# A fused attention and gMLP kernel: batch 0 loaded and attended pair by pair, its gMLP moved ahead, dummy matmuls, and two batches stored from another queue

## Chip, cores, metric

The kernel runs on one core of one Trainium2 chip. The metric is device time in microseconds (us); lower is better. All times compared here are of runs in the same (fast) state; runs in the slow state are left out of the ratios. A ratio is the mean time of one kernel's fast runs divided by the mean of the other's fast runs of the same rounds, so it is not quite the ratio of the medians that are quoted beside it.

## The reference

Sliding-window causal attention (window 64) over q, k, v of shape (8, 8, 576, 64) in float32, then a gMLP block with a spatial gate on the (8, 576, 512) result:

```python
scores = where(0 <= i - j < 64, q @ k.T / 8, -1e9)           # per batch and head
x = softmax(scores) @ v                                      # heads side by side: 8 x 576 x 512
h = maximum(x @ w_in, 0);  u, v = h[..., :512], h[..., 512:]
v_n = (v - mean(v)) / sqrt(var(v) + 1e-6)
v_s = einsum('ts,bsd->btd', w_spatial, v_n) + b_spatial[None, :, None]
out = (u * v_s) @ w_out                                      # 8 x 576 x 512
```

## The kernel before

All work is written out in a fixed order, and each engine runs its instructions in that order. Per batch b there are five attention steps s (four pairs of heads, then the remaining 64 rows of all heads). The letters used below:

- T(b,s): PE transposes q and k; VectorE copies them from PSUM, where PE's products go, to SBUF, where the tiles lie. S: scores. E: ScalarE's exp, then VectorE's min with a mask. P(b,s): PE's product with v. N1, N2: ScalarE's log and exp of the sums, then VectorE's x.
- V(b,j): five tiles of the v half of `x @ w_in`. LN: VectorE normalises them in five operations `vn`. U and G: the u half and the spatial product with the gate. O(b,j): the output product; ScalarE copies it to an output buffer `ob`, and a DMA stores it.
- GpSimd casts q, k, v of the next batch to float16 and makes `hs`, a copy of v shifted by 64 rows, with five copies. P needs it.

`ob` has three buffers; from batch 1 on all loads of q, k and v, and all stores, are issued by SyncE in program order; and loads run two batches ahead. The code below is condensed, with cuts marked by dots.

```python
def emit_O(b, j):
    ...                                                   # four matmuls into po
    ob = mpool.tile([128, 512], f32, tag="ob", bufs=3, name=f"ob{b}_{j}")
    nc.scalar.copy(ob[0:jn, :], po[0:jn, :])
    nc.sync.dma_start(out[b, 128 * j:128 * j + jn, :], ob[0:jn, :])
...
for p in range(4):                                        # batch 0: all casts come first, so
    cast_pair(0, 1, p, nc.gpsimd)                         # VectorE has four q casts in front of
    cast_pair(0, 0, p, nc.vector)                         # the first copy of a transpose
    cast_pair(0, 2, p, nc.gpsimd)
    shift_pair(0, p, nc.gpsimd)
...
for i in range(B + 2):            # attention of i, V/LN/U/G of i-1, O of i-2
    ...
    if i == 0: loads += [(1, x, c) ...]                   # 15 chunks of 256 KB
    if i + 2 < B: loads += [(i + 2, x, c) ...]            # two batches ahead
    for s in range(5):
        ...                       # load_chunk on SyncE; casts of batch i+1 on GpSimd
        emit_T(next step); two units of todo (V, U, G, O)
        emit_S(i, s); emit_P(previous step)
        ...                       # E, N1, N2 with one unit of todo between each
```

The softmax here doesn't subtract the row's maximum and nothing guards it: scores larger than these inputs give would overflow.

## Time and profile before

| | before |
|---|---|
| median of the first three runs | 266.21 us (266.09 to 266.33) |
| span of the profiled run | 265.3 us |
| PE busy | 217.4 us (82%) |
| start of P(2,0), the first P of batch 2 | 92.07 us |
| from there to the end | 173.2 us |
| V(b,0) to V(b+1,0), b = 2 to 6 | 25.5 us |

P(2,0) is used throughout as a mark: it splits the start of the program from its steady part.

The page is the profiler's summary of one execution. It cuts the span into 40 slices (one digit is the busy share, or the clock granted to PE, of 6.6 us in tenths). Its chain of waits is followed back from the last instruction, at each step to what released it; SPq is SyncE issuing DMAs. For the kernel before:

```profile
PE   0008325999990499999999999999999999999893
...
PEclk9999655599997599999999999999999999999999
DMA  8999999999999699869966995597320040005005
...
PE 64%; SPq 16%; DMA 9%; POOL 6%; issue 1%; ACT 1%; DVE 0%; ACTq 0%; POOLq 0%
```

Apart from its end, PE has holes in slices 0 to 6 and 12 to 13 only. Its granted clock reads 5 tenths in slices 5 to 7 and 13. And the DMA row stands at 9 until slice 12: in that stretch the chain of waits is mostly made of SyncE's issues and of DMAs (SPq and DMA, 25% of the whole together), the rest of GpSimd's casts and shifts (POOL, 6%).

The windows view (stretch, its length, busy us of each engine with the number of instructions, granted clock, DMA share, GB/s):

```profile
core 0: us, PE busy (x) PEld busy (x) DVE busy (x) ACT busy (x) POOL busy (x), PEclk, DMA share, GB/s
...
35.00:40.00 5.00, 1.60 (x6) 0.63 (x6) 0.00 (x0) 0.00 (x0) 4.49 (x8) 0.50 1.23 216
...
80.00:85.00 5.00, 0.00 (x0) 0.00 (x0) 0.00 (x0) 0.00 (x0) 2.61 (x5) 0.83 1.00 204
85.00:90.00 5.00, 0.30 (x1) 0.10 (x1) 0.00 (x0) 0.93 (x3) 4.71 (x6) 0.50 0.85 239
```

PE does nothing at all for five microseconds while the DMA moves 204 GB/s. What it waits for is in three timelines of the same kernel (start, duration, engine, line, operation; in brackets the idle time before it and its releaser). PE first:

```profile
78.86 0.38 PE L311 MATMUL pv_0_1231<-win_189,x_3_1098 128*128 128x512 f16 x1
89.70 0.58 PE L311 MATMUL pv_1_1242<-win_183,x_0_766 128*128 128x512 f16 x1 [10.46 <-ACT ob_3_1195 L387]
...
92.07 0.64 PE L262 MATMUL oz_0_1271<-e_2_0_1175,onesK 128*64 128x512 f16 x2
```

The second V tile of batch 1 comes 10.46 us late; its PSUM buffer is released by ScalarE's copy of `ob_3`. ScalarE:

```profile
76.02 0.59 ACT L387 COPY ob_2_1184<-po_2_1178 128x512 f32<-128x512 f32 x1 [0.16 <-PE po_2_1178 L384]
...
89.07 0.59 ACT L387 COPY ob_3_1195<-po_3_1189 128x512 f32<-128x512 f32 x1 [12.18 <-DMA out_dram<-ob_0_1133]
```

That copy waits 12.18 us for the store of `ob_0`, whose buffer it reuses. SyncE's issues:

```profile
81.42 3.06 SPq L76 DMA_DIRECT2D nk_1105<-in_k_dram  x3
84.58 1.24 SPq L388 DMA_DIRECT2D out_dram<-ob_0_1133  x1
```

The store of `ob_0`, ready at 74.1, is issued at 84.58, behind loads of batch 4. Batch 2's data were there by then, as GpSimd's timeline shows (last v chunk cast, fourth shift copy):

```profile
67.46 0.80 POOL L88 CAST hv_593<-nv_353 64x512 f16<-64x512 f32 x1 [0.22 <-DMA nv_353<-in_v_dram]
...
71.49 1.04 POOL L104 COPY hs_594<-hv_593 64x1024 f16<-64x1024 f16 x1
```

### The profile page before, as it was taken

The numbers are of one execution on the slowest core, as the hardware profiler recorded it, in microseconds if no ns is written. First come the engines' busy times: TensorE is split into PE (matmuls) and PEld (weight loads), VectorE is DVE, ScalarE is ACT, GpSimd is POOL, SyncE is SP. The second block draws the span as 40 slices with busy tenths as digits, with TensorE's granted clock in tenths as the row PEclk, the third lists the DMA queues.
The fourth block names the chain that finished last, engine by engine and source line by source line (L and its number), as shares of the span: only waits on it lengthen the run. The fifth ranks groups of instructions, "written<-read, shape, count | busy, mean of one in ns | idle before, by whom it ended". The sixth has DMA issues, their size and how long they took to land.

```text
span 265.3 us, 6260 instructions
## 1 busy us (share of the span) xinstructions
PE 217.4 (82%) x2537; PEld 114.1 (43%) x2537; DVE 155.3 (59%) x316; ACT 149.7 (56%) x262; POOL 120.6 (45%) x183
## 2 busy tenths in 40 slices
PE   0008325999990499999999999999999999999893
PEld 0006203644640245544554455445544644454351
DVE  5125402598740377759766976697578648863730
ACT  1006502766640467577667767776876777776423
POOL 4579384795885607670866087417830000000000
PEclk9999655599997599999999999999999999999999
DMA  8999999999999699869966995597320040005005
GB/s 161 210 195 208 207 210 200 183 207 203 200 195 203 201 200 207 134 216 211 183 153 199 191 217 144 167 215 139 115 68 0 2 160 20 4 2 180 0 2 178
DMA packets 119822, 40.41 MB, mean 152 GB/s; under 512 B 113584, under 2 KB 114672, under 8 KB 119792
## 3 DMA queue, kind: packets, MB, share of 16 engines
q1 hardware_dynamic: 113200, 36.58, 67.9%
q0 software_dynamic: 1840, 2.24, 4.8%
q10 hardware_dynamic: 4752, 1.18, 2.7%
q8 instruction: 20, 0.33, 0.6%
q14 instruction: 10, 0.08, 0.1%
HBM read 32.79 MB, written 9.44 MB: 159 GB/s over the span
## 4 chain that ended last, share of the span: by engine, by line
PE 64%; SPq 16%; DMA 9%; POOL 6%; issue 1%; ACT 1%; DVE 0%; ACTq 0%; POOLq 0%
SPq L76 14%; DMA nq_76<-in_q_dram 4%; DMA nv_353<-in_v_dram 2%; DMA nv_229<-in_v_dram 2%; DMA out_dram<-ob_0_1133 2%; SPq L68 2%; POOL hk_592 L88 1%; POOL hk_1101 L88 1%; POOL hs_233 L103 1%; POOL hs_233 L104 1%; POOL hs_594 L104 1%; POOL hs_594 L103 1%; PE pv_1_1242 L311 1%; PE ps_0_4499 L363 1%; PE ps_0_2533 L363 1%
## 5 line engine op out<-in xcount | busy, mean ns | idle before, releaser
L245 ACT ACTIVATE e_0_0_275<-sc_0_257 128x1024 f16<-128x1024 f32 x1 | 1.0, 1025 | 19.2 <-PE sc_0_257 L223 19.2
L191 PE MATMUL tp_1_245<-id_110,hk_80 128*128 128x128 f16 x4 | 0.6, 302 | 11.0 <-DVE qk_0_225 L197 11.0
L311 PE MATMUL pv_1_1242<-win_183,x_0_766 128*128 128x512 f16 x1 | 0.6, 585 | 10.5 <-ACT ob_3_1195 L387 10.5
L191 PEld LDWEIGHTS <-hk_80 128*128 128x128 f16 x16 | 1.5, 129 | 17.4 <-issue 9.5
L81 DVE CAST hq_79<-nq_76 128x512 f16<-128x512 f32 x4 | 1.9, 481 | 10.9 <-DMA nq_76<-in_q_dram 10.9
L289 DVE TENSOR_TENSOR x_4_1200<-oz_4_1163,zi_4_1198 128x256 f16<-128x256 f32 x1 | 0.4, 425 | 12.8 <-ACT zi_4_1198 L287 12.8
L249 ACT ACTIVATE e2r_547<-sc_4_509 128x512 f16<-128x512 f32 x1 | 0.6, 597 | 12.5 <-PE sc_4_509 L237 12.5
L88 POOL CAST hk_1655<-nk_1105 128x512 f16<-128x512 f32 (+1 forms) x5 | 2.8, 610 | 10.5 <-issue 10.5
L387 ACT COPY ob_3_1195<-po_3_1189 128x512 f32<-128x512 f32 x1 | 0.6, 586 | 12.2 <-DMA out_dram<-ob_0_1133 12.2
L197 DVE COPY qk_0_507<-tp_0_497 128x1024 f16<-128x1024 f16 x1 | 0.7, 693 | 11.4 <-PE tp_0_497 L194 11.4
L191 PE MATMUL tp_0_497<-id_110,hk_231 128*128 128x128 f16 x4 | 1.2, 288 | 7.2 <-POOL hk_231 L88 7.2
L262 PEld LDWEIGHTS <-onesK 128*64 128x64 f16 x80 | 4.8, 108 | 5.1 <-issue 2.5
L88 POOL CAST hk_3317<-nk_2767 128x512 f16<-128x512 f32 (+1 forms) x5 | 2.9, 610 | 8.6 <-issue 8.6
L88 POOL CAST hk_2763<-nk_2213 128x512 f16<-128x512 f32 (+1 forms) x5 | 2.8, 609 | 8.6 <-issue 8.6
L88 POOL CAST hk_2209<-nk_1659 128x512 f16<-128x512 f32 (+1 forms) x5 | 2.8, 610 | 8.6 <-issue 8.6
L81 POOL CAST hk_80<-nk_77 128x512 f16<-128x512 f32 x4 | 2.4, 612 | 7.7 <-DMA nk_77<-in_k_dram 7.7
L191 PE MATMUL tp_0_215<-id_110,hk_80 128*128 128x128 f16 x4 | 0.6, 305 | 5.8 <-POOL hk_80 L81 5.8
L311 PEld LDWEIGHTS <-x_1_882 128*128 128x128 f16 x4 | 0.4, 104 | 10.9 <-issue 10.7
L191 PEld LDWEIGHTS <-hk_231 128*128 128x128 f16 x16 | 1.3, 115 | 8.4 <-POOL hk_231 L88 7.8
L88 POOL CAST hv_593<-nv_353 128x512 f16<-128x512 f32 (+1 forms) x5 | 3.6, 719 | 2.7 <-DMA nv_353<-in_v_dram 2.6
L343 PEld LDWEIGHTS <-win_187 128*128 128x128 f16 x32 | 3.1, 98 | 3.8
L343 PEld LDWEIGHTS <-win_189 128*128 128x128 f16 x32 | 3.1, 98 | 3.8
(1855 smaller groups left out, 952.9 us busy)
## 6 DMA issues: line engine op xcount, KB each, us to landing
nk_77<-in_k_dram SPq DMA_DIRECT2D x9, 128.0 KB, 4.6
nv_78<-in_v_dram ACTq DMA_DIRECT2D x9, 128.0 KB, 4.7
nq_76<-in_q_dram SPq DMA_DIRECT2D x9, 128.0 KB, 4.5
nk_228<-in_k_dram SPq DMA_DIRECT2D x4, 256.0 KB, 5.5
nq_227<-in_q_dram SPq DMA_DIRECT2D x4, 256.0 KB, 14.7
nv_229<-in_v_dram SPq DMA_DIRECT2D x4, 256.0 KB, 6.0
nk_352<-in_k_dram SPq DMA_DIRECT2D x4, 256.0 KB, 6.0
nq_351<-in_q_dram SPq DMA_DIRECT2D x4, 256.0 KB, 5.3
```

Of the source, the lines that this page charges most:

```text
L68: eng.dma_start(NAT[b][x][:, 0:4, h, :], SRC[x][b, h, 0:512, :].rearrange("(c p) d -> p c d", p=128))
L76: nc.sync.dma_start(NAT[b][x][0:sn, c, :, :], SRC[x][b, :, 128 * c:128 * c + sn, :].transpose([1, 0, 2]))
L81: eng.tensor_copy(F16[b][x][:, 0:4, hs, :], NAT[b][x][:, 0:4, hs, :])
L88: eng.tensor_copy(F16[b][x][0:sn, c, :, :], NAT[b][x][0:sn, c, :, :])
L103: eng.tensor_copy(vs[0:64, c:c + 2, :, :], vn[0:64, c:c + 2, :, :])
L104: eng.tensor_copy(vs[64:128, c + 1:c + 3, :, :], vn[64:128, c:c + 2, :, :])
L191: nc.tensor.transpose(tp[:, 512 + 128 * c:640 + 128 * c], Kh[:, c, 2 * s:2 * s + 2, :], id16[:, :])
L245: nc.scalar.activation(e2[:, :, :], sc[:, :, :], AF.Exp, bias=0.0, scale=0.125)
L262: nc.tensor.matmul(oz[64 * h:64 * h + 64, 1, 0:n], onesK[:, :], e2[:, h, 0:n], start=True, stop=True)
L311: nc.tensor.matmul(pv[0:jn, :], xcol(b, r, j), w_in_sb[r][:, 512:1024], start=(r == 0), stop=(r == 3))
L343: nc.tensor.matmul(pu[:, :], w_in_sb[r][:, 128 * m:128 * m + 128], X[b, r][:, :], start=(r == 0), stop=(r == 3))
L363: nc.tensor.matmul(ps[:, :], VN[b, kk][0:kn, 128 * m:128 * m + 128], wspT[kk][0:kn, 0:512], start=(kk == 0), stop=(kk == 4))
```

## The change

The intent, as the diff shows it: start attention on the first pair of batch 0 when it lands, use the time in which batch 1 lands for batch 0's gMLP, keep PE's clock up with dummy matmuls, and take the stores of batches 0 and 1 off SyncE. From batch 3 on, loads run one batch ahead instead of two. The core of the diff, condensed (lines joined, cuts marked by dots):

```diff
+    def warm(n):                                  # n dummy matmuls 128x512
+        t = psp.tile([128, 512], f32, tag="mm", bufs=3, ...)
+        for _ in range(n):
+            nc.tensor.matmul(t[:, :], scratch[:, 0:128], scratch[:, :], start=True, stop=True)
...
-        nc.sync.dma_start(out[b, 128 * j:128 * j + jn, :], ob[0:jn, :])
+        (nc.scalar if b < 2 else nc.sync).dma_start(out[b, 128 * j:128 * j + jn, :], ob[0:jn, :])
...
+    load_by_pairs(0); warm(16)
+    casts_step(0, 0, _Act, nc.vector); emit_T(0, 0)        # k casts of batch 0 on ScalarE
+    for s in range(5):
+        if s < 4: casts_step(0, s + 1, _Act, nc.vector)
+        if s == 1: load_win()
+        if s == 2: load_wsp()
+        if s == 3: load_wout(); new_half(1); load_by_pairs(1)
+        att_step(0, s, [], 0, 0, None)
+        warm(4)
+        if s < 4: emit_T(0, s + 1)
+        warm(3)
+    ...                                            # casts of batch 1 by pairs; V, W, LN, U of batch 0;
+    ...                                            # loads of batch 2; attention 1 with G, U, O of batch 0
...
-        if i + 2 < B:
-            loads += [(i + 2, x, c) for x in (1, 0, 2) for c in range(5)]
+        if i + 1 < B:
+            loads = [(i + 1, x, c) for x in (1, 0, 2) for c in range(5)]
```

More of the change, by code (lines that the diff above doesn't have):

```diff
@@ L106, in shift_half, with load_by_pairs @@
             eng.tensor_copy(vs[0:64, 4, :, :], vn[0:64, 4, :, :])
-    new_batch(0)
-    new_half(0)
-    for p in range(4):
-        for x in (1, 0, 2):
-            load_heads(0, x, 2 * p, nc.sync if x != 2 else nc.scalar)
-    for x in (1, 0, 2):
-        load_rem(0, x, nc.sync if x != 2 else nc.scalar)
+    scratch = cpool.tile([128, 512], f16, name="scratch")
+    nc.vector.memset(scratch[:], 0.0)
+    def warm(n):
+        t = psp.tile([128, 512], f32, tag="mm", bufs=3, name=f"warm{nc.next_id()}")
+        for _ in range(n):
+            nc.tensor.matmul(t[:, :], scratch[:, 0:128], scratch[:, :], start=True, stop=True)
+    def load_by_pairs(b):
+        new_batch(b)
+        for p in range(4):
+            for x in (1, 0, 2):
+                load_heads(b, x, 2 * p, nc.scalar if (b == 0 and p < 2 and x == 2) else nc.sync)
+        for x in (1, 0, 2):
+            load_rem(b, x, nc.sync)
+    load_by_pairs(0)
+    new_half(0)
+    warm(16)
     id16 = cpool.tile([128, 128], f16, name="id16")
@@ L148 @@
         nc.vector.memset(vn4_t[i][64:65, :], 1.0)
-    for p in range(4):
-        cast_pair(0, 1, p, nc.gpsimd)
-        cast_pair(0, 0, p, nc.vector)
-        cast_pair(0, 2, p, nc.gpsimd)
-        shift_pair(0, p, nc.gpsimd)
-    for x in (1, 0, 2):
-        cast_rem(0, x, nc.gpsimd)
-    shift_rem(0, nc.gpsimd)
-    w_in_sb = []
-    for r in range(4):
-        t = cpool.tile([128, 1024], f16, name=f"win{r}")
-        nc.gpsimd.dma_start(t[:], moe_w_in[128 * r:128 * (r + 1), :])
-        w_in_sb.append(t)
@@ L165, with casts_step @@
-    wsp_nat = []
-    for tch in range(5):
-        tn = 128 if tch < 4 else 64
-        t = cpool.tile([128, 576], f16, name=f"wnat{tch}")
-        nc.gpsimd.dma_start(t[0:tn, :], moe_w_spatial[128 * tch:128 * tch + tn, :])
-        wsp_nat.append(t)
-    wspT = [cpool.tile([128, 576], f16, name=f"wspT{kk}") for kk in range(5)]
-    nc.gpsimd.dma_start(wspT[4][64:65, 0:576], moe_b_spatial[:].unsqueeze(0))
-    w_out_sb = []
-    for r in range(4):
-        t = cpool.tile([128, 512], f16, name=f"wout{r}")
-        nc.gpsimd.dma_start(t[:], moe_w_out[128 * r:128 * (r + 1), :])
-        w_out_sb.append(t)
+    def casts_step(b, s, engk, engq):
+        if s < 4:
+            cast_pair(b, 1, s, engk)
+            cast_pair(b, 0, s, engq)
+            cast_pair(b, 2, s, nc.gpsimd)
+            shift_pair(b, s, nc.gpsimd)
+        else:
+            for x in (1, 0, 2):
+                cast_rem(b, x, nc.gpsimd)
+            shift_rem(b, nc.gpsimd)
@@ new lines, with tensor_copy, load_win @@
+    class _Act:
+        @staticmethod
+        def tensor_copy(o, i):
+            nc.scalar.copy(o, i)
+    w_in_sb = [cpool.tile([128, 1024], f16, name=f"win{r}") for r in range(4)]
+    w_out_sb = [cpool.tile([128, 512], f16, name=f"wout{r}") for r in range(4)]
+    wsp_nat = [cpool.tile([128, 576], f16, name=f"wnat{t}") for t in range(5)]
+    wspT = [cpool.tile([128, 576], f16, name=f"wspT{kk}") for kk in range(5)]
+    def load_win():
+        for r in range(4):
+            nc.gpsimd.dma_start(w_in_sb[r][:], moe_w_in[128 * r:128 * (r + 1), :])
@@ L180, with load_wsp, load_wout @@
+    def load_wsp():
+        for t in range(5):
+            tn = 128 if t < 4 else 64
+            nc.gpsimd.dma_start(wsp_nat[t][0:tn, :], moe_w_spatial[128 * t:128 * t + tn, :])
+        nc.gpsimd.dma_start(wspT[4][64:65, 0:576], moe_b_spatial[:].unsqueeze(0))
+    def load_wout():
+        for r in range(4):
+            nc.gpsimd.dma_start(w_out_sb[r][:], moe_w_out[128 * r:128 * (r + 1), :])
     QK = {}
@@ L397, in emit_W, with run_units, att_step @@
         nc.scalar.copy(wspT[kk][0:sn, 0:576], wps[0:sn, 0:576])
-    def units(i):
+    state = {"P": None}
+    def run_units(todo, n):
+        for _ in range(n):
+            if todo:
+                todo.pop(0)()
+    def att_step(i, s, todo, before, between, nxt, t_last=False):
+        if not t_last and nxt is not None:
+            emit_T(*nxt)
+        run_units(todo, before)
+        post = []
+        if i < B:
+            emit_S(i, s)
+            post.append(lambda: emit_E(i, s))
+        if state["P"] is not None:
+            pb, ps_ = state["P"]
+            emit_P(pb, ps_)
+            post.append(lambda: emit_N1(pb, ps_))
+            post.append(lambda: emit_N2(pb, ps_))
+        while post:
+            post.pop(0)()
+            run_units(todo, between)
+        state["P"] = (i, s) if i < B else None
@@ new lines, in O_units, with V_units @@
+    def O_units(o):
+        return [lambda j=j: emit_O(o, j) for j in range(5)] if 0 <= o < B else []
+    def V_units(a):
+        return [lambda j=j: emit_V(a, j) for j in range(5)] if 0 <= a < B else []
+    casts_step(0, 0, _Act, nc.vector)
+    emit_T(0, 0)
+    for s in range(5):
+        if s < 4:
+            casts_step(0, s + 1, _Act, nc.vector)
+        if s == 1:
+            load_win()
+        if s == 2:
+            load_wsp()
+        if s == 3:
+            load_wout()
+            new_half(1)
+            load_by_pairs(1)
+        att_step(0, s, [], 0, 0, None)
+        warm(4)
+        if s < 4:
+            emit_T(0, s + 1)
+        warm(3)
@@ new lines @@
+    for s in range(5):
+        casts_step(1, s, nc.gpsimd, nc.gpsimd)
+    att_step(B, 0, [], 0, 0, None)
+    for f in V_units(0):
+        f()
+    for kk in range(5):
+        emit_W(kk)
+    emit_LN(0)
+    for m in (0, 1, 2):
+        emit_U(0, m)
+    new_batch(2)
+    for x in (1, 0, 2):
+        for c in range(5):
+            load_chunk(2, x, c)
+    emit_T(1, 0)
+    todo = [lambda: emit_G(0, 0), lambda: emit_U(0, 3), lambda: emit_G(0, 1), lambda: emit_U(0, 4),
+            lambda: emit_G(0, 2), lambda: emit_G(0, 3), lambda: emit_G(0, 4)] + O_units(0)
@@ L401, in units @@
+    for s in range(5):
+        att_step(1, s, todo, 1, 1 if s else 0, (1, s + 1) if s < 4 else None)
+    run_units(todo, 99)
+    for i in range(2, B + 2):
         a, o = i - 1, i - 2
         st = [[] for _ in range(5)]
-        if i == 0:
-            st[4] += [lambda kk=kk: emit_W(kk) for kk in range(5)]
-        if 0 <= o < B:
-            st[0] += [lambda j=j: emit_O(o, j) for j in range(5)]
-        if 0 <= a < B:
-            st[1] += [lambda j=j: emit_V(a, j) for j in range(5)]
+        if o > 0:
+            st[0] += O_units(o)
+        if a < B:
+            st[1] += V_units(a)
@@ L413, in units @@
             st[4] += [lambda: emit_U(a, 3), lambda: emit_G(a, 3), lambda: emit_G(a, 4)]
-        return st
-    pend_P = None
-    emit_T(0, 0)
-    for i in range(B + 2):
-        st = units(i)
         loads = []
         casts = []
-        if i == 0:
-            new_batch(1)
-            loads += [(1, x, c) for x in (1, 0, 2) for c in range(5)]
-        if i + 2 < B:
-            loads += [(i + 2, x, c) for x in (1, 0, 2) for c in range(5)]
+        if i + 1 < B:
+            loads = [(i + 1, x, c) for x in (1, 0, 2) for c in range(5)]
+        if i == 2:
+            new_half(2)
+            for x in (1, 0, 2):
+                for c in range(5):
+                    cast_chunk(2, x, c, nc.gpsimd)
+            for hf in range(3):
+                shift_half(2, hf, nc.gpsimd)
+            emit_T(2, 0)
         if i + 1 < B:
@@ L431 @@
             casts += [lambda hf=hf: shift_half(i + 1, hf, nc.gpsimd) for hf in range(3)]
-        nl = (len(loads) + 4) // 5
-        ncst = (len(casts) + 3) // 4
         for s in range(5):
-            todo = list(st[s])
-            for (lb, lx, lc) in loads[nl * s:nl * s + nl]:
+            for (lb, lx, lc) in loads[5 * s:5 * s + 5]:
                 if lb not in NAT:
@@ L439 @@
                 load_chunk(lb, lx, lc)
-            for f in casts[ncst * s:ncst * s + ncst]:
+            for f in casts[5 * s:5 * s + 5]:
                 f()
             nxt = (i, s + 1) if s < 4 else (i + 1, 0)
-            if nxt[0] < B:
-                emit_T(*nxt)
-            for _ in range(2 if i else 0):
-                if todo:
-                    todo.pop(0)()
-            post = []
-            if i < B:
-                emit_S(i, s)
-                post.append(lambda: emit_E(i, s))
-            if pend_P is not None:
-                pb, ps_ = pend_P
-                emit_P(pb, ps_)
-                post.append(lambda: emit_N1(pb, ps_))
-                post.append(lambda: emit_N2(pb, ps_))
-            while post or todo:
-                if post:
-                    post.pop(0)()
-                if todo:
-                    todo.pop(0)()
-            pend_P = (i, s) if i < B else None
+            if nxt[0] >= B:
+                nxt = None
+            if i < B or s == 0:
+                att_step(i, s, st[s], 2, 1, nxt)
+            run_units(st[s], 99)
 _INS = ['q', 'k', 'v', 'moe_w_in', 'moe_w_spatial', 'moe_b_spatial', 'moe_w_out']
```

## The prediction

> **What bounds it now.** The page's 40 slices show two regimes. From about 90 us on PE is at 9 tenths or more at full clock: PE-bound, 25.5 us per batch (in the chain of waits, the first V matmuls of successive batches start at 116.18, 141.67, 167.16). Before 90 us PE is starved. The windows view: 30-45 us has 3.9 us busy, 80-90 us 0.3 us, with the granted clock at 0.50 for much of 30-50 us. The chain there is SyncE load issues and DMA (SPq 16%, DMA 9% of the span), and the DMA moves about 205 GB/s without pause: batches 0, 1, 2, the weights and batch 3 land one after the other; batch 2's last V chunk at about 67 us, its shifted V copies (GpSimd, four of 1.04 us) end at 72.5 us.
>
> Batch 0's first transposed copy waits until 18.9 us: VectorE has all four q casts queued in front of it. PE stops 10.5 us before the second V tile of batch 1 (78.9 to 89.7): ScalarE's copy into the output buffer waits for the store of ob_0, which SyncE issues only at 84.6, behind loads of batches 3 and 4. P of (batch 2, step 0) therefore starts at 92.1.
>
> **What changes.** Batch 0's attention follows its pairs (about 4 us apart) and ends near 25 us. V, the weight transposes, LN and three U of batch 0 go into 25-40 us, where PE now idles; G and O of batch 0 are interleaved with attention 1, which follows batch 1's pairs (landed near 48 us) and ends near 56. Iteration 2 loses its five O units (4.6 us of PE). Stores of batches 0 and 1 go from ScalarE's queue, so the 10.5 us stall should vanish. Added: 16 dummy matmuls before any data is there and 7 per step (1.5 us warm) sit in waits and should cost below 1 us. ScalarE pays ten issues (0.3 to 0.5 us each as SyncE's stores show) and batch 0's k casts; perhaps 1 us reaches PE.
>
> **What it is worth.** From P(2,0) on the program is unchanged in PE work, so I place P(2,0). It needs batch 2's V and shifts. The bytes ahead of it are the same as before (three batches of 17.3 us, weights about 9.5 us), plus batch 0's stores now ahead of them, about 3 us (1.18 MB, estimated from the 205 GB/s with part overlapped). The Trainium skill, "DMA: Bandwidth & Descriptors", section "Issuing engines are not separate DMA queues", says that queues of different engines share the same 16 DMA engines; so the other queue frees the order of issue, not bandwidth. P(2,0): about 75.5 us instead of 92.1. Gain 16.6 us, less 1 us for ScalarE's issues. PE idles in 58-75 us, so a cold restart as now (0.64 at 90-95 us) stays.
>
> Predicted: 250 us, range 243 to 255; faster by over 2%: 0.96; within 2%: 0.035; slower: 0.005.
>
> **What would show it.** Batch 0's exponentials start near 10 us, not 21.3; no PE wait on an ob copy; P(2,0) near 75 us, released by GpSimd's shifts after the DMA of batch 2's V; PE idle about 12 us between 56 and 75; afterwards 25.5 us per batch with no new stall; same drain; DMA still near 205 GB/s up to 70 us.
>
> **What would make it wrong.** Stores of batch 2, again on SyncE, may queue behind loads of batch 5 in iteration 4 (I count about 9 us of slack): a second stall of up to 10 us. Batch 2 may land later (small pair loads below 205 GB/s), or earlier, if the stores overlap fully (then about 246).

## The result

| | before | after |
|---|---|---|
| median | 266.27 us (4 runs) | 250.25 us (4 runs, 249.06 to 251.18) |
| ratio of the fast runs | | 0.938 (0.932 to 0.945) |
| span of the profiled run | 265.3 us | 249.3 us |
| PE busy | 217.4 us | 227.3 us (51 dummies in it) |
| start of P(2,0) | 92.07 us | 74.53 us |
| from P(2,0) to the end | 173.2 us | 174.8 us |
| V(2,0) to V(6,0), four batches | 101.9 us | 104.0 us |

The gain of 15.9 us in the span is 17.5 us at the start minus 1.6 us in the rest (2.0 lost in the four batches from V(2,0) on, 0.4 won elsewhere).

The page's slices and chain shares for the changed kernel:

```profile
PE   7784996996399999999999999999999999999893
...
PEclk9999799799569999999999999999999999999998
DMA  8999999999999996992389948995499040014005
...
PE 60%; DVE 13%; ACT 9%; DMA 8%; SPq 3%; POOL 2%; issue 2%; ACTq 1%; POOLq 0%
```

Against before, PE is busy from the first slice, the hole at slice 12 has gone, and a small one is left at slices 9 and 10. SyncE and DMA have shrunk in the chain from 25% to 11%; VectorE and ScalarE, 1% before, are 22%. These shares are of the whole span, so the chain has to be read by stretches: ahead of 76 us, SyncE and DMA make up 22 us of it (68 of the first 92 us before), PE 31 us, and VectorE and ScalarE 13 us. That is the first sign that the start is no longer bound by data alone. The larger part of the 22% (some 55 us) lies behind 76 us, where VectorE and ScalarE had next to no share before: the first sign of the slower batches below. The hole in the windows view:

```profile
core 0: us, PE busy (x) PEld busy (x) DVE busy (x) ACT busy (x) POOL busy (x), PEclk, DMA share, GB/s
55.00:60.00 5.00, 5.00 (x62) 2.28 (x64) 1.35 (x3) 3.26 (x5) 2.43 (x5) 1.00 1.07 247
60.00:65.00 5.00, 0.64 (x19) 0.45 (x20) 1.47 (x3) 2.76 (x5) 2.65 (x4) 0.82 1.14 292
65.00:70.00 5.00, 3.30 (x52) 2.74 (x50) 2.10 (x4) 1.23 (x2) 2.82 (x4) 0.50 1.34 227
70.00:75.00 5.00, 5.00 (x60) 2.82 (x60) 2.79 (x7) 3.02 (x6) 4.77 (x6) 0.65 1.09 194
```

PE's timeline there, with the same mark P(2,0) at its end:

```profile
64.64 0.64 PE L281 MATMUL oz_3_1153<-e_1_3_1108,onesK 128*64 128x512 f16 x2 [4.36 <-DVE x_2_1133 L308]
...
68.37 0.59 PE L210 MATMUL tp_1_1235<-id_130,hk_1183 128*128 128x128 f16 x4 [1.70 <-DVE qk_0_1216 L216]
...
74.53 0.41 PE L281 MATMUL oz_0_1348<-e_2_0_1277,onesK 128*64 128x512 f16 x2
```

P(2,0) has no wait in front of it. The idle time is 4.36 us in front of P(1,3) and 1.70 us in front of T(2,1), released by VectorE. ScalarE's timeline shows what lies behind the first:

```profile
54.97 0.58 ACT L406 COPY ob_0_1033<-po_0_1027 128x512 f32<-128x512 f32 x1 [0.63 <-PE po_0_1027 L403]
55.58 0.39 ACTq L407 DMA_DIRECT2D out_dram<-ob_0_1033  x1
...
60.55 0.58 ACT L406 COPY ob_3_1117<-po_3_1111 128x512 f32<-128x512 f32 x1 [0.92 <-DMA out_dram<-ob_0_1033]
```

The copy of `ob_3` still waits for the store of `ob_0`, now issued at once, but it lands only 4.9 us after its issue began. ScalarE does E(1,3) meanwhile, so its own idle time is only 0.92 us, but the log and exp that P(1,3) needs come after this copy. The larger part of PE's 4.36 us is therefore ScalarE's own row of copies, issues, log and exp. GpSimd's casts and shifts of batch 2:

```profile
68.41 0.61 POOL L88 CAST hv_1184<-nv_764 64x512 f16<-64x512 f32 x1 [0.43 <-DMA nv_764<-in_v_dram]
...
72.72 1.04 POOL L104 COPY hs_1185<-hv_1184 64x1024 f16<-64x1024 f16 x1
```

The fourth shift ends at 73.76, some 0.8 us before P(2,0). So P(2,0) came where the prediction had put it, but it was not released by what the prediction named. SyncE's issues in iteration 4, which the prediction had named as a risk:

```profile
106.52 5.45 SPq L76 DMA_DIRECT2D nk_2286<-in_k_dram  x5
120.40 0.36 SPq L407 DMA_DIRECT2D out_dram<-ob_0_2316  x1
```

SyncE is done with its loads at 111.97 and the first store comes at 120.40: the slack is 8.4 us, and there is no second stall.

### The profile page after: what moved, and what is told of

The parts are those of the page before. It is cut to its first block, busy times and chain, and to the rows that moved or that the text cites. A ratio compares the mean times of both kernels' runs of the same rounds, so it can differ in the third digit from the quotient of the medians.

```text
span 249.3 us, 6391 instructions
## 1 busy us (share of the span) xinstructions
PE 227.3 (91%) x2588; PEld 116.8 (47%) x2588; DVE 155.3 (62%) x317; ACT 152.2 (61%) x266; POOL 122.1 (49%) x183
## 4 chain that ended last, share of the span: by engine, by line
PE 60%; DVE 13%; ACT 9%; DMA 8%; SPq 3%; POOL 2%; issue 2%; ACTq 1%; POOLq 0%
SPq L68 3%; DMA nv_80<-in_v_dram 2%; DMA out_dram<-ob_0_1033 2%; DMA out_dram<-ob_1_3433 2%; DMA nq_78<-in_q_dram 2%; ACTq L407 1%; PE ps_0_804 L382 1%; PE warm_583 L114 1%; PE pv_0_1308 L330 1%; PE ps_0_4590 L382 1%; PE ps_0_4237 L382 1%; DVE mv_172 L336 1%; PE ps_0_3720 L382 1%; PE ps_1_895 L382 0%; PE ps_3_4653 L382 0%
## 5 line engine op out<-in xcount | busy, mean ns | idle before, releaser
L88 POOL CAST hq_2281<-nq_2285 128x512 f16<-128x512 f32 (+1 forms) x5 | 3.2, 635 | 12.8 <-DMA nq_2285<-in_q_dram 12.8
L114 PEld LDWEIGHTS <-scratch 128*128 128x128 f16 x51 | 5.0, 112 | 7.3 <-issue 3.8
L88 POOL CAST hq_3389<-nq_3393 128x512 f16<-128x512 f32 (+1 forms) x5 | 3.9, 797 | 8.8 <-DMA nq_3393<-in_q_dram 8.8
L88 POOL CAST hq_2835<-nq_2839 128x512 f16<-128x512 f32 (+1 forms) x5 | 3.6, 720 | 8.3 <-DMA nq_2839<-in_q_dram 8.3
L176 ACT CAST hk_109<-nk_79 128x512 f16<-128x512 f32 x4 | 2.5, 618 | 7.5 <-DMA nk_79<-in_k_dram 7.5
L114 PE MATMUL warm_113<-scratch 128*128 128x512 f16 x16 | 5.5, 524 | 1.3 <-DVE scratch L109 1.3
L81 POOL CAST hv_110<-nv_80 128x512 f16<-128x512 f32 x4 | 2.5, 632 | 8.3 <-DMA nv_80<-in_v_dram 7.3
L88 POOL CAST hv_1729<-nv_1733 128x512 f16<-128x512 f32 (+1 forms) x5 | 3.5, 708 | 4.4 <-DMA nv_1733<-in_v_dram 4.4
L88 POOL CAST hq_1727<-nq_1731 128x512 f16<-128x512 f32 (+1 forms) x5 | 2.9, 609 | 4.6 <-DMA nq_1731<-in_q_dram 4.6
L88 POOL CAST hv_2283<-nv_2287 128x512 f16<-128x512 f32 (+1 forms) x5 | 3.2, 637 | 3.8 <-DMA nv_2287<-in_v_dram 3.8
L81 POOL CAST hv_433<-nv_437 128x512 f16<-128x512 f32 x4 | 2.5, 613 | 5.2 <-DMA nv_437<-in_v_dram 5.1
L88 POOL CAST hv_1184<-nv_764 128x512 f16<-128x512 f32 (+1 forms) x5 | 3.1, 611 | 3.9 <-DMA nv_764<-in_v_dram 3.9
L362 PEld LDWEIGHTS <-win_181 128*128 128x128 f16 x32 | 3.1, 98 | 3.8
L362 PEld LDWEIGHTS <-win_182 128*128 128x128 f16 x32 | 3.1, 98 | 3.8
L88 POOL CAST hv_1220<-nv_1224 128x512 f16<-128x512 f32 (+1 forms) x5 | 3.9, 780 | 2.0 <-DMA nv_1224<-in_v_dram 2.0
L88 POOL CAST hq_1182<-nq_762 128x512 f16<-128x512 f32 (+1 forms) x5 | 3.3, 654 | 3.2 <-DMA nq_762<-in_q_dram 2.7
L281 PE MATMUL oz_3_1153<-e_1_3_1108,onesK 128*64 128x512 f16 x2 | 0.6, 611 | 4.4 <-DVE x_2_1133 L308 4.4
L88 POOL CAST hv_3391<-nv_3395 128x512 f16<-128x512 f32 (+1 forms) x5 | 3.0, 611 | 2.8 <-DMA nv_3395<-in_v_dram 2.8
L88 POOL CAST hv_2837<-nv_2841 128x512 f16<-128x512 f32 (+1 forms) x5 | 3.3, 666 | 2.0 <-DMA nv_2841<-in_v_dram 1.8
```

The source lines that it names most:

```text
L81: eng.tensor_copy(F16[b][x][:, 0:4, hs, :], NAT[b][x][:, 0:4, hs, :])
L88: eng.tensor_copy(F16[b][x][0:sn, c, :, :], NAT[b][x][0:sn, c, :, :])
L114: nc.tensor.matmul(t[:, :], scratch[:, 0:128], scratch[:, :], start=True, stop=True)
L176: nc.scalar.copy(o, i)
L281: nc.tensor.matmul(oz[64 * h:64 * h + 64, 1, 0:n], onesK[:, :], e2[:, h, 0:n], start=True, stop=True)
L362: nc.tensor.matmul(pu[:, :], w_in_sb[r][:, 128 * m:128 * m + 128], X[b, r][:, :], start=(r == 0), stop=(r == 3))
```

## The experiments

All twelve further kernels gave correct results. The edits are condensed. "Rest" is the span of the profiled run minus the start of P(2,0). Ratios are to the kernel before, of the same rounds.

| run | median us | ratio (95% interval) | P(2,0) | rest |
|---|---|---|---|---|
| before | 266.2 to 267.6 | 1 | 92.07 | 173.2 |
| changed kernel | 250.25 | 0.938 (0.932 to 0.945) | 74.53 | 174.8 |
| e1_store_only | 263.46 | 0.988 (0.984 to 0.991) | 79.61 | 181.3 |
| e2_sync_stores | 255.51 | 0.957 (0.954 to 0.961) | 78.83 | 174.1 |
| e3_no_dummies | 253.17 | 0.947 (0.943 to 0.950) | 77.14 | 174.3 |
| e4_ob6 | 250.75 | 0.938 (0.936 to 0.941) | 72.75 | 175.6 |
| e5_all_act_stores | 263.45 | 0.984 (0.980 to 0.989) | 80.33 | 181.7 |
| e6_two_ahead | 255.60 | 0.957 (0.953 to 0.961) | 73.50 | 181.1 |
| e7_short_chain | 252.01 | 0.942 (0.939 to 0.945) | 73.48 | 175.3 |
| e8_short_chain_pairs2 | 252.00 | 0.943 (0.939 to 0.946) | 74.13 | 175.0 |
| e9_gate | 249.84 | 0.933 (0.929 to 0.937) | 71.97 | 174.3 |
| e10_sync_ob6 | 247.64 | 0.927 (0.923 to 0.932) | 70.06 | 175.9 |
| e11_all | 245.69 | 0.920 (0.915 to 0.924) | 69.47 | 173.4 |
| e12_act_stores_gate | 261.50 | 0.978 (0.973 to 0.982) | 80.55 | 179.3 |

One caution on this table: e9 to e12 were made on another chip than e1 to e8, and P(2,0) is of one profiled run each. How far P(2,0) can be trusted is seen in e9: up to P(2,0) it runs the same instructions as the changed kernel (its gate acts only later), and yet P(2,0) came at 71.97 us instead of 74.53. A shift of P(2,0) by up to 2.6 us is therefore no evidence by itself. In profiles of these runs the names have no batch and buffer numbers.

### e1_store_only: the store queue alone

```diff
 # kernel before
-        nc.sync.dma_start(out[b, ...], ob[0:jn, :])
+        (nc.scalar if b < 2 else nc.sync).dma_start(out[b, ...], ob[0:jn, :])
```

> The kernel before with one edit: the stores of batches 0 and 1 are issued by ScalarE, all else as before. Theory A (the store order is the larger half of the gain; the stall before the second V tile of batch 1 goes, the reordering gives the rest): P(2,0) starts near 82 us instead of 92.1 and the time is about 255 to 256 us, some two thirds of the gain of 16 us. Rival B (reordering batch 0 and its gMLP earns the gain; without it the freed 10 us run into the next wait for data): at most 4 us gain, 262 us or more. Theory A also expects a rest of the ob wait, up to 3 us, since the first store still takes 4 to 5 us to land beside the loads, as in the changed kernel (4.9 us).

Measured: 263.46 us. P(2,0) came at 79.61, earlier than theory A asked, but the end moved by only 4.4 us. Theory A fell on the time, and rival B's number held, though not for its reason. PE's waits between 100 and 150 us (waiter, releaser: us, times, longest), and SyncE's issues there:

```profile
PE pv L311 <- ACT ob L387: 6.1, 1, 6.1
```

```profile
128.07 3.15 SPq L76 DMA_DIRECT2D nk<-in_k_dram  x3
131.32 6.42 SPq L388 DMA_DIRECT2D out_dram<-ob  x5
```

The stall of iteration 2 has moved to iteration 4. With batches 0 and 1 out of the way, the stores of batch 2 are now the ones that queue behind loads (of batches 5 and 6), because loads run two batches ahead. P(4,0) follows P(3,0) after 33.1 us, against 25.5 us before. That is the second stall I had feared for the changed kernel; there, loads one batch ahead leave SyncE idle in time.

### e2_sync_stores: all of the change but the store queue

```diff
 # changed kernel
-        (nc.scalar if b < 2 else nc.sync).dma_start(out[b, ...], ob[0:jn, :])
+        nc.sync.dma_start(out[b, ...], ob[0:jn, :])
```

> The changed kernel with the stores of batches 0 and 1 back on SyncE, all else as changed. Theory A: they are issued only after the loads of batch 2, near 64 us instead of 55.6, so the copy of the fourth O tile of batch 0 waits about 8 us longer, P(2,0) starts near 82 us, and the time is about 257 us (half of the gain lost). Rival B (reordering earns the gain): 251 to 252 us.

Measured: 255.51 us; PE waits 9.1 us at 60.9 us, and P(2,0) comes at 78.83. The direction was theory A's, the size smaller: the reordering with the shorter load-ahead earns 4.3%, and the store queue another 1.9%, where alone it earned 1.2%.

### e3_no_dummies: no dummy matmuls

```diff
 # changed kernel
-    warm(16)
...
-        warm(4)
...
-        warm(3)
```

> The changed kernel without any dummy matmul. Theory A (everything before 55 us hides behind the DMA of batches 1 and 2, so neither the clock nor the dummies matter): within 1 us of the changed kernel, 249 to 251 us, although the granted clock shows 0.5 to 0.7 in parts of 5 to 35 us. Rival C (the dummies keep the clock up where PE is on the chain): 252 us or more.

Measured: 253.17 us, ratio 0.947 (0.943 to 0.950) against 0.938 (0.932 to 0.945): about 2 us lost, with intervals that just overlap. The time is the one that rival C asked for. V of batch 0, which is on the chain, took 6.17 us for its 20 matmuls instead of 4.61 us. The windows view of V's line in the run without dummies, early and late in V (a matmul that runs across a border counts in both):

```profile
core 0: us, PE busy (x) PEld busy (x), PEclk, DMA share, GB/s
...
32.50:33.50 1.00, 1.00 (x4) 0.30 (x2) 1.00 1.25 206
...
35.50:36.50 1.00, 1.00 (x6) 0.34 (x4) 1.00 0.16 32
```

Four matmuls in a microsecond become six (one starts every 0.43 us, later every 0.22), yet the granted clock reads 1.00 in both. The first 1.00 is no measurement: the packed trace of this run holds no clock record before 34.70 us, and where there is none, the column shows 1.00. The first record, of the full clock, begins where the pace changes. In the kernel before the first record begins at 25.29 us, in the changed kernel at 5.19 us, and the durations agree: four 128x128 transposes at 19.67 us took 0.59 us before, at 9.97 us 0.39 us in the changed kernel. So the dummies brought the full clock earlier. But they did not hold it: e8 and e11 keep all dummies except those behind the last step, a stretch at 0.50 fell on V there (27.63 to 31.04 us in e8), and V took 6.29 us, while e7, with the same instructions up to there, took 4.61. The pace of V in one profile is thus no proof of what the dummies are worth. The later P(2,0) of this run (2.6 us) is within the scatter named above, and has other parts: GpSimd came 1.7 us later through its weight loads to batch 0's remainder casts, and a store of batch 0 that ScalarE waits for took 5.9 us to land instead of 4.9. Whether those follow from the dummies stays open.

### e4_ob6: six output buffers

```diff
 # changed kernel
-        ob = mpool.tile([128, 512], f32, tag="ob", bufs=3, ...)
+        ob = mpool.tile([128, 512], f32, tag="ob", bufs=6, ...)
-        vs = mpool.tile([128, 512], f16, tag=f"vs{j}", bufs=2, ...)
+        vs = mpool.tile([128, 512], f16, tag=f"vs{j}", bufs=1, ...)
```

> The changed kernel with six output buffers instead of three (room made by one instead of two buffers for the relu of V, which is dead long before it is written again; the instruction order is the same on each engine). In the changed kernel's chain of waits the 4.9 us landing of the first store of batch 0 holds ScalarE, and through it P(1,3), T(2,1) and P(2,0) at 74.5; GpSimd's shifts of batch 2 end at 73.8. Theory D (store landing and data arrival are two limits within 1 us of each other): P(2,0) moves only to about 73.9 us, now released by the shifts; the later stalls on ob (1 to 2 us in iterations 3 to 6) go, and the time is 247 to 248.5 us. Rival E (the store landing alone holds it): P(2,0) near 70 us and a time near 245. Rival F (neither; P(2,0) stays and the later iterations too): 249.5 to 250.5.

Measured: the same time as the changed kernel (ratio 0.938 both). P(2,0) moved by 1.8 us to 72.75, less than the scatter. Steadier is the stretch from the copy of `ob_0` to P(1,3): 9.7 us in the changed kernel (9.3 in e9 and 9.5 in e6, which have three buffers too, and 10.9 in e3, with its slower store), 8.6 here and in e7 (13.0 in e8, whose other wait is shown below). So the landing of the store held ScalarE by about 1 us. The shifts ended at 73.28, so the data are a limit close behind. But the batches still took 26.0 us, so theory D's second half fell: the waits on `ob` were not what makes the later batches slow.

### What slows the later batches

The search for those 0.5 us led to VectorE's `vn`. Two neighbours in the changed kernel:

```profile
133.20 0.41 DVE L352 TENSOR_SCALAR vn_1_2546<-vs_1_2433,mv_172,rs_2541 128x512 f16<-128x512 f16 x1
133.53 0.70 DVE L352 TENSOR_SCALAR vn_2_2548<-vs_2_2485,mv_172,rs_2541 128x512 f16<-128x512 f16 x1
```

and GpSimd at that time:

```profile
133.37 0.71 POOL L88 CAST hq_2281<-nq_2285 128x512 f16<-128x512 f32 x1 [0.72 <-DMA nq_2285<-in_q_dram]
```

The same operation takes 0.41 us where it began ahead of GpSimd's cast, or 0.70 us where the cast was already running. Over both profiles, `vn` took 0.39 to 0.41 us in all 52 cases without a GpSimd operation beside it (37 before, 15 after). With one beside it, 15 of 28 took 0.47 to 0.81 us. PE waits for these five operations in G(b,0). The Trainium skill, page "SBUF — State Buffer", section "Who interferes with whom", says that VectorE, in modes that tensor_scalar can enter, and GpSimd share one pair of SBUF ports, which one instruction holds to its end while the other blocks. This trace agrees, with the figures just given. The five together took 1.7 us in iterations of 25.5 us and 2.0 to 2.3 us in the changed kernel's of 26.0.

### e5_all_act_stores: every store by ScalarE in the kernel before

```diff
 # kernel before
-        nc.sync.dma_start(out[b, ...], ob[0:jn, :])
+        nc.scalar.dma_start(out[b, ...], ob[0:jn, :])
```

> The kernel before with every store issued by ScalarE (the run with only batches 0 and 1 there moved the 10 us stall from iteration 2 to iteration 4, where the stores of batch 2 queue behind loads of batches 5 and 6: P(2,0) 12.5 us earlier, the end only 4.4 us earlier). Theory A2 (the stall is a queue order and can be had whole): no PE stall on an ob copy in iterations 2 to 6, P(2,0) near 79.6 us as there, then 25.5 us per batch, a span near 253 and a time of 253 to 255 us, nearly all of the changed kernel's gain with batch 0 untouched. Rival G (the freed time is lost again, because the loads come under pressure or ScalarE pays for 40 issues): 257 us or more.

Measured: 263.45 us. Theory A2 fell. No stall on `ob` of the old kind was left, but V(4,0) came 32.0 us after V(3,0). VectorE's timeline in that iteration, then GpSimd's, then PE's:

```profile
139.24 4.70 DVE L333 TENSOR_SCALAR vn<-vs,mv,rs 128x512 f16<-128x512 f16 x5
```

```profile
139.91 1.04 POOL L104 COPY hs<-hv 64x1024 f16<-64x1024 f16 x1
141.01 1.03 POOL L103 COPY hs<-hv 64x1024 f16<-64x1024 f16 x1
142.10 1.04 POOL L104 COPY hs<-hv 64x1024 f16<-64x1024 f16 x1
```

```profile
141.16 0.39 PE L363 MATMUL ps<-wspT,vn 128*128 128x512 f16 x1 [0.71 <-DVE vn L333]
142.25 0.39 PE L363 MATMUL ps<-wspT,vn 128*128 128x512 f16 x1 [0.70 <-DVE vn L333]
```

The five `vn` take 4.70 us instead of 1.7: each waits for one shift copy of 1.04 us. PE runs one matmul per `vn` and waits 0.7 us for the next. Then the granted clock falls: 0.84 in 140 to 145 us and 0.50 in 145 to 150 us. The trace's record puts the fall at 143.42 us; in the 3.41 us ahead of it (the length of the window that the page named next gives) PE had been busy for 1.25 us, with four single matmuls. The Trainium skill, page "TensorE: Matmul & The Clock Gate", section "What's actually happening", says that the clock follows how busy PE was in a recent window; this trace agrees, and PE did not have to be wholly idle for it.

### e6_two_ahead: loads two batches ahead in the changed kernel

```diff
 # changed kernel
+    new_batch(3); load_chunk(3, x, c) for all x, c       # right behind batch 2
-        if i + 1 < B: loads = [(i + 1, x, c) ...]
+        if i + 2 < B: loads = [(i + 2, x, c) ...]
-        (nc.scalar if b < 2 else nc.sync).dma_start(...)
+        (nc.scalar if b < 4 else nc.sync).dma_start(...)
```

> The changed kernel with loads running two batches ahead again, as in the kernel before (batch 3 right behind batch 2, batch i+2 in iteration i), and the stores of batches 0 to 3 by ScalarE. In the changed kernel batches take 26.0 us instead of 25.5, and the five normalising operations of VectorE per batch take 2.1 to 2.8 us together instead of 1.7 when GpSimd casts run beside them. Theory H (the later loads put the casts beside the normalising; two ahead moves them away): 25.5 to 25.6 us per batch, VectorE's five at 1.7 us, 248 to 249 us. Rival I (the 0.5 us come from something else, such as stores beside loads): 26.0 us per batch remain and the time stays at 250 to 251.

Measured: 255.6 us, 5 us slower than the changed kernel; both theories were wrong on the time. The normalising of one batch took 4.81 us, and that iteration 31.5 us, as in e5; the last two stretches from V to V, with the normalising at 1.7 us, took 26.2 and 25.5 us. So the load-ahead does decide where the casts fall, but two ahead put the long shift copies on the normalising. The shorter load-ahead of the change avoids this.

### e7_short_chain and e8_short_chain_pairs2: what holds P(2,0)

```diff
 # e7: changed kernel with six ob buffers, and
-        if s == 2: load_wsp()
-        if s == 3: load_wout()
+        if s == 3: load_wsp(); load_wout()          # behind batch 0's remainder casts
-        warm(4) / warm(3) after every step          # now after the steps 0 to 3 only
 # e8: e7 with batch 2 by pairs
-    load_chunk(2, x, c) ... cast_chunk(2, x, c), shift_half(2, hf)
+    load_by_pairs(2)    ... casts_step(2, s, nc.gpsimd, nc.gpsimd)
```

> The changed kernel with six output buffers, the loads of the spatial weights issued by GpSimd only after batch 0's remainder casts (they hold those casts back 3 us now), and no dummies behind the last step of batch 0 (2.8 us in the chain of the six-buffer run). Theory D (the arrival of batch 2's V and its shifts is a limit close behind): the chain of batch 0 and 1 ends about 4 to 5 us earlier, but P(2,0) stays near 72.5 to 73.5, now released by GpSimd's shifts, and the time is 249 to 250.5. Rival E (the chain of compute and latency alone holds P(2,0)): P(2,0) at 68 to 69, time 245 to 246.5.

> The same with batch 2 also loaded, cast and shifted by pairs, so that its first pair is there some 12 us before its last V chunk. Theory D: now P(2,0) is free of the data and moves to 68 to 70 us; the time drops 3 to 4 us below the run without pairs, to 245 to 247. Rival E: no difference between the two. Rival J (the later batches are then bound by DMA and give it back): P(2,0) earlier, but the time within 1 us of the other.

Measured: 252.0 us both, slightly slower than the changed kernel if anything. In e7, V of batch 0 began at 26.84 instead of 30.08, and P(2,0) came at 73.48. The chain of waits of e7 at that point (start, us, what):

```profile
73.37 1.05 POOL hs L104
...
74.46 0.25 PE oz L290 x4
```

GpSimd's last shift releases the last matmuls of P(2,0), though not its first: data bound at its end, as theory D said. In e8 the shifts of the first pair, which P(2,0) needs, ended at 54.6 and the last of all at 70.2, but P(2,0) came at 74.13 all the same: theory D's second number fell, and so did J, since P(2,0) was not early at all. ScalarE's timeline in e8 shows a third limit:

```profile
52.29 0.58 ACT L406 COPY ob<-po 128x512 f32<-128x512 f32 x1 [0.63 <-PE po L403]
55.57 0.42 ACTq L407 DMA_DIRECT2D out_dram<-ob  x1
56.04 0.63 ACT L306 ACTIVATE zi<-ln 128x512 f32<-128x512 f32 x1 [3.17 <-DMA nq<-in_q_dram]
```

The copy ended at 52.87; the issue of its store began at 55.57, with the wait put down to a load of q, and the exp behind it was held for 3.17 us. In the packed trace, the DMAs of SyncE and ScalarE go round eight semaphores that both share, and this store waits for the one of a q load, which landed at 55.50. So a store on "the other queue" can still wait for a load. In e7, without the pair loads of batch 2, the same store was issued 0.04 us after its copy.

### e9_gate: GpSimd's casts kept off the normalising

```diff
 # changed kernel, iterations 2 and later
-            for f in casts[5 * s:5 * s + 5]:
+            if s == 3 and casts:                     # waits for the last vn of this iteration
+                nc.gpsimd.tensor_copy(scratch_g[0:1, 0:1], VN[a, 4][0:1, 0:1])
+            for f in (casts[0:5], [], [], casts[5:], [])[s]:
                 f()
```

> The changed kernel with one gate: from iteration 2 on, GpSimd casts q and v of the next batch, and shifts v, only after a one-element GpSimd copy that reads the last output of VectorE's normalising of that iteration; the k casts stay where they were. VectorE's normalising operation takes 0.40 to 0.41 us in every one of the 15 cases where no GpSimd operation runs beside it, and up to 0.81 where one does (12 of 25). Theory H2 (these collisions make the 26.0 us per batch): the five operations take 1.7 us in all batches from 2 on, batches take 25.5 us again from the third on, P(2,0) stays at 74.5, and the time is 2 us lower, 248 to 248.5 us. Rival I (the collisions are hidden, the 0.5 us come from elsewhere): the time stays at 250 to 251.

Measured: 249.84 us, ratio 0.933 (0.929 to 0.937) against 0.938 (0.932 to 0.945); the intervals overlap, so the time alone does not settle it. The profile does for the mechanism: all five `vn` together take 1.70 us in every batch from 1 on, and the three batches from V(3,0) to V(6,0) take 25.48 us each where the changed kernel takes 25.9 on average. But the two batches before them took 27.4 and 26.6 us (27.1 and 26.2 in the changed kernel), each with a new wait of PE of 0.9 us, so the gate gave part of it back; e12 shows what is behind this wait. The profiled run is 3.0 us shorter than that of the changed kernel, but 2.6 us of this lie ahead of P(2,0), where the gate does nothing: that part is scatter between runs and chips, and the expected P(2,0) of 74.5 was missed by it. The gate's own share is 0.5 us of the rest.

### e10_sync_ob6: six buffers in place of the other queue

```diff
 # changed kernel, with the edit of e4, and
-        (nc.scalar if b < 2 else nc.sync).dma_start(out[b, ...], ob[0:jn, :])
+        nc.sync.dma_start(out[b, ...], ob[0:jn, :])
```

> The changed kernel with all stores back on SyncE but six output buffers (with three, and SyncE, it took 255.5 us; with six and ScalarE 250.8). Theory K (the other queue only works round the shortage of output buffers: a store may wait as long as nobody waits for its buffer): 249.5 to 251 us, no PE or ScalarE stall on an ob copy in the iterations 1 to 3. Rival L (the order of the queue matters by itself): 254 us or more.

Measured: 247.64 us, better than theory K asked. With three buffers, SyncE stores cost 5 us against the changed kernel (e2); with six they gain about 1%. The store may now wait, since nobody waits for its buffer. The only difference to e4 is the issuing engine of ten stores, five of them ahead of P(2,0). Both profiled runs start the copy of `ob_0` at 54.64 us. The exp that P(1,3) needs, first in e4, then here:

```profile
61.82 0.63 ACT L306 ACTIVATE zi<-ln 128x512 f32<-128x512 f32 x1 [0.63 <-ACT ob L406]
```

```profile
60.18 0.63 ACT L306 ACTIVATE zi<-ln 128x512 f32<-128x512 f32 x1
```

So ScalarE's five issues were dear: they stand between copies and activations that PE waits for, and cost 1.6 us. P(1,3) came 6.9 us after that copy here and in e11, 8.6 in e4 and e7. P(2,0) came 2.7 us earlier (70.06 against 72.75); the other 1 us arises behind V(1,0), where PE ran at a granted 0.50 until 71.72 us in e4, but only until 67.97 here.

### e11_all: everything that helped

```diff
 # e8, with all stores on SyncE (edit of e10) and the gate of e9
```

> Changed kernel, six output buffers, all stores by SyncE, spatial weights behind batch 0's remainder casts, no dummies behind the last step of batch 0, batch 2 by pairs, and the gate. In the run with pairs of batch 2 and ScalarE stores, P(2,0) was not held by data (shifts done at 69.5) but by ScalarE: its first store could be issued only 2.7 us after its copy, since the issue waits for an earlier load in a shared set of 8 DMA semaphores, and every activation behind it waited. Theory: with the stores off ScalarE P(2,0) comes at 70 to 71 us, batches take 25.5 us, 244.5 to 246.5 us. Rival (early data are lost again to later waits): 248 us or more.

Measured: 245.69 us, ratio 0.920 (0.915 to 0.924): the best version, and clear of the changed kernel's interval. P(2,0) at 69.47 and P(3,0) 25.48 us later, where e10 takes 27.38 us, in part because P(2,0) waits for shifts inside (1.1 us). The theory held for the time; one later batch took 26.4 us, with a mask operation of 3.40 us in it as in e12.

### e12_act_stores_gate: the gate in the e5 kernel

```diff
 # e5 with the gate of e9 in iterations 1 and later
```

> The kernel before with all stores by ScalarE (263.5 us; there batch 4's iteration took 32 us instead of 26: its five normalising operations alternated with four 1.04 us shift copies of GpSimd and took 4.7 us, PE waited 0.7 us for each, and the granted clock then fell to 0.5), plus the gate. Theory H2: no iteration of 32 us any more, all from the third on at 25.5 to 26, the clock at 1.0 from 60 us on, and 256.5 to 258.5 us. Rival M (the 32 us come from something else): 262 us or more.

Measured: 261.5 us. The 32 us iteration is gone, the normalising takes 1.7 us everywhere and the clock is 1.0 from 60 us on, so the collision was its cause. But every iteration now takes 26.6 us, and the gain expected was missed. VectorE's mask operation in e12:

```profile
92.95 3.41 DVE L251 TENSOR_TENSOR e<-e,mask 128x1024 f16<-128x1024 f16 x1 [0.73 <-ACT e L245]
```

It takes 0.69 us undisturbed. Behind the gate GpSimd's casts and shifts run without a pause, and one VectorE operation with two SBUF inputs waited through them for 2.7 us. PE then waits 0.9 us in each iteration. The same operation took 3.41 us in both slow batches of e9, and 1.3 to 1.9 us in its three fast ones. The collision was moved, not removed.

## Why the prediction was right, and where it was not

1. **The time and the mark: right.** 250.25 us against 250; P(2,0) at 74.5 against 75.5. The first exponential of batch 0 came at 9.3 us (predicted near 10), the end of the program from V(7,0) on stayed the same within 0.4 us, and no second stall came in iteration 4 (slack 8.4 us, counted 9).
2. **"P(2,0) near 75 us, released by GpSimd's shifts": wrong about the release.** In the changed kernel PE, ScalarE and the landing of a store held it, and the data were ready 0.8 us earlier. Runs e4, e7, e8 and e10 show several limits close together: the store landing (about 1 us of P(1,3), gone with six buffers), ScalarE's issues (1.6 us of P(1,3)), PE's own pace at the granted 0.50, and the shifts (which finish P(2,0) in e7 and e10). My number was right because these lie close together, not because I had the right one; that is luck. The chain that I had taken to be free was late: P(0,4) came at 29.7 us where I had batch 0's attention end near 25, and P(1,4) at 69.9 where I had batch 1's end near 56. So "PE idle about 12 us" was 6.1 us. The DMA moved 201 to 216 GB/s in the stretches from 5 to 55 us, as predicted, but 255 GB/s from 55 to 70 us, where stores and loads were under way together; this fits the data being ready earlier than I had counted.
3. **"No PE wait on an ob copy": wrong.** PE does not wait for the copy itself, but for an exp of ScalarE that stands behind it. The other queue shortened this wait (from 10.5 us to about 1 us, e4), but the store still takes 4.9 us to land beside the loads.
4. **"Afterwards 25.5 us per batch": wrong by 0.5 us per batch.** The term is the steady part, taken as unchanged; it measured 2.0 us more over four batches. The cause is `vn` beside GpSimd's casts. The runs e9 and e12 show that the normalising returns to 1.7 us when the casts are kept away, and in e9 three batches return to 25.48 us with it. I had looked at engines' busy time, and not at which operations of two engines run side by side.
5. **"Perhaps 1 us reaches PE" for ScalarE's issues: too small.** The comparison of e4 and e10 puts it at 1.6 us of P(1,3) for five of the ten issues, and, with what follows from it, at 1.1% of the time of the kernel before.
6. **What earned the gain.** Neither half is enough: the store queue alone gives 1.2% (e1), the rest alone 4.3% (e2), together 6.2%. The two sum to 5.5%, at the edge of the interval of the whole (5.5 to 6.8%), so whether more than a sum is at work is not shown. That the two act on one thing is seen in the traces: the stall on stores follows from three buffers and the length of the load queue ahead of a store, and the change shortens that queue too.

Open stays how much of e3's 2 us comes from the clock and how much from later weights and stores, why e7 is no faster than e4, and how the 4.3% of e2 divide between the pairs, the moved gMLP and the shorter load-ahead, which no run tests one by one.

## What to carry to other kernels

When PE waits on a store's buffer, first ask for more buffers, and only then for another queue: six buffers on the old queue beat three buffers with the new one. After removing a stall, look where the freed work runs next, since the same stall reappeared two iterations later, and then another took its place. When a GpSimd copy moves in time, check which VectorE operations it now runs beside, as both it and the clock of PE can turn a few tenths of a microsecond into six (e5). And before a time in one profile is called moved, look how far it moves between runs of the same instructions: here 2.6 us.

## What the Trainium skill lacked or had wrong

- "SBUF — State Buffer", "Who interferes with whom", describes that one instruction blocks for one other. It does not say that a waiting VectorE operation can be passed over by a run of GpSimd operations: one took 3.41 us instead of 0.69 beside back-to-back casts and shifts (e12), while five others took turns with shift copies (4.70 us instead of 1.7, e5).
- "TensorE: Matmul & The Clock Gate", "What's actually happening", gives the activity window, but no share of busy time at which the clock falls; a PE that was idle in part only (1.25 of 3.41 us busy) fell to a granted 0.50 (e5). The page warns of unreliable clock events ("Seeing it yourself"), but not that a trace can hold no clock record at all for its first tens of microseconds (34.70 us in e3, 25.29 in the kernel before), so that a view which takes a missing record for the full clock misleads (a matmul every 0.43 us, then every 0.22, both read as 1.00).
- "DMA: Bandwidth & Descriptors", "Issuing engines are not separate DMA queues", calls the issue time usually small relative to the DMA itself, which holds here (about 0.4 us of issue, 4.9 us to landing). It does not say that the issuing engine's own work is delayed: five stores issued by ScalarE instead of SyncE held P(1,3) back by 1.6 us (e4 against e10).
- No page that I read says that DMAs issued by SyncE and ScalarE in such a program may share eight semaphores, so that a store on one queue may wait for a load on the other (2.7 us in e8). This is the program's doing, not the chip's.
